# A fused linear-attention and mixer kernel: seven weight shifts written in place, loads and ranks in a new order

## The chip, the cores and the metric

One NeuronCore of a Trainium2 chip runs the whole program. The time is device microseconds of that core, lower is better. The engines are TensorE (PE, with its weight loads listed as PEld), VectorE (DVE), ScalarE (ACT), GpSimd (POOL) and SyncE (SP), which here only issues DMAs. Each engine runs its own instructions strictly in the order in which the program was written; engines wait for each other by semaphores.

## The reference

Batch 4, 4 heads, 1088 positions, head dimension 32. A linear attention with a product feature map of 8 x 8 = 64 features is followed by a token mixer and a channel mixer:

```
phi(x) = outer(S1 x, S2 x)                         # 64 features of q and of k
x   = (phi(q) @ (phi(k)^T v)) / (phi(q) @ sum_s phi(k) + 1e-6)     # [B, 1088, 128]
u   = x + (relu(x^T @ w_tok1) @ w_tok2)^T          # token mixer, 256 hidden
out = u + relu(u @ w_ch1) @ w_ch2                  # channel mixer, 1536 hidden
```

Data are float32; S1, S2 and the four weights arrive as float64 words (two 32 bit words each) and are turned into float32 on the chip.

## The kernel before, in words

**Conversion of weights.** Each weight is cut into pieces: w00 to w04 (w_tok1), w10 to w15 (w_tok2), w20 to w22 (w_ch1), w30 to w32 (w_ch2), seventeen in all, and `s` for S1 and S2. `convert` makes float32 from a piece in six operations: `.abs` (ACT, L363, high word into a buffer `c`), `.low` (ACT, L367, low word into `tail`), `.clamp` (DVE, L370, `c` to `c`), `.shift` (DVE, L374, `c` shifted left by 3 and masked, into a PSUM bank of the pool `ps_h`), `.merge` (DVE, L377, puts the sign bit in, from the high word and the PSUM bank back to `c`), and `.add` (POOL, L381 and L383, `c` plus `tail`). Pieces of w_tok are kept as `whole`; each piece is then split into a high half (`.hi`, ACT, L474) and a low half (`.lo`, POOL or DVE, L477), so that TensorE can work with three fast products in place of one slow one. `c` and `tail` have four buffers each, `ps_h` three banks, which the channel mixer uses too.

**Batches.** For each batch b: keys `K` (projection L504, feature products k_p on DVE L534, sums with v L551, block matrix `kvz` L561), queries `Q` (batch 0 on PE, L642; later ones through DRAM, L697, L714 to L740), attention and token mixer `A` (L760 and the division L768 to L778; L816 or L822 with w_tok1; the relu `h` L834; its transposition L856; the residual L847; L938 or L942 with w_tok2; `uh` and `ul`, the halves of u, L913 and L916). In batch 0 the token mixer uses `whole` float32 weights, later batches the halves.

**Channel mixer.** `U0` to `U11` are spans of up to 384 positions. For each span and each of 12 hidden blocks: three matmuls with w_ch1 into a `ps_h` bank (L992), the relu on ACT (`hh`, L996), the rest of it on DVE (`hl`, L999), three matmuls with w_ch2 into a `ps_o` bank (L1005). These 144 blocks are most of the time.

**What sets the order.** The operations are put into a list with names (`w13.clamp`, `K1.s`, `U0.h`); `Plan.run` walks through them with a rough cost for each and gives the next one on whichever engine is free to the operation of the highest level. The level is the cost of all that depends on it plus a number of its own from the table `LEAD` (in ns). Loads are issued by SP in the order of `LOADS`. Where it believes PE idle, the program puts in matmuls of an identity (`fill`, L342) whose results nobody reads. An operation with `port=True` is kept apart in this plan from POOL's operations; that concerns the plan alone, on the chip the engines' queues and semaphores decide.

Of the kernel before, what the change touches and what calls it, by code (L numbers as in the profile page):

```python
# [11 lines left out]
I32 = mybir.dt.int32  # L12
# [18 lines left out]
TILES = tuple((t * P, P) for t in range(NT))  # L31

CUTS = {0: (2, 2, 2, 2, 1), 2: (4, 4, 4), 3: (4, 4, 4)}
LOADS = "k0 q0 00 v0 01 02 03 04 10 11 20 30 q1 12 13 k1 21 31 v1 14 15 22 32".split()


WIDE = 384
# [2 lines left out]
def _spans():  # L40
# [22 lines left out]
KEYS_ON_POOL = set()  # L63

LEAD = {
    "A0.d2": -161700.0,
    "A0.u0": -740800.0,
    "A0.w2": 67900.0,
    "A1.n2": 62000.0,
    "A1.x": 384700.0,  # L70
    "A1.xT3": 472400.0,
    "A2.w0": -38700.0,
    "A2.w1": -1729700.0,
    "A3.w2": -107200.0,
    "K0.kvz": -142200.0,
    "K0.s08": -237500.0,
    "K1.s": -160000.0,
    "K1.v0": 40800.0,
    "K3.c0": 99700.0,
    "K3.p": 103300.0,  # L80
    "K3.s": -300900.0,
    "K3.v4": -498400.0,
    "Q0.a10": 1269000.0,
    "Q0.a20": 461800.0,
    "Q1.m00": -332100.0,
    "Q1.m10": -30800.0,
    "Q1.p": 115700.0,
    "Q3.p": -1683600.0,
    "U0.f": 988300.0,
    "U0.h": 359200.0,  # L90
    "U0.l": -79900.0,
    "U1.f": 653600.0,
    "U11.f": 345700.0,
    "U2.f": 96300.0,
    "U2.l": -115500.0,
    "U2.s": -804700.0,
    "U4.l": 520500.0,
    "U5.s": -35900.0,
    "U6.s": -144500.0,
    "U8.s": -175400.0,  # L100
    "w00.hi": -357200.0,
    "w00.lo": -624600.0,
    "w00.low": 15500.0,
    "w01.add": -162900.0,
    "w01.hi": -266600.0,
    "w01.lo": -1103500.0,
    "w02.hi": -337700.0,
    "w02.lo": -1981200.0,
    "w03.hi": -871700.0,
    "w03.lo": -604900.0,  # L110
    "w03.low": 376600.0,
    "w03.shift": -580100.0,
    "w04.abs": 1406800.0,
    "w04.add": 140400.0,
    "w04.hi": -260600.0,
    "w04.lo": -663100.0,
    "w04.low": 1049700.0,
    "w10.abs": 830500.0,
    "w10.hi": -265000.0,
    "w10.low": 172800.0,  # L120
    "w10.shift": -115500.0,
    "w11.abs": 656200.0,
    "w11.clamp": -128400.0,
    "w11.low": -9800.0,
    "w12.abs": 1523900.0,
    "w12.clamp": -157100.0,
    "w12.hi": -811900.0,
    "w12.lo": -452800.0,
    "w12.low": 1313100.0,
    "w13.abs": 945800.0,  # L130
    "w13.clamp": -534800.0,
    "w13.hi": 621700.0,
    "w13.low": -19300.0,
    "w13.merge": 637100.0,
    "w13.shift": -290300.0,
    "w14.lo": -1439000.0,
    "w14.low": -519800.0,
    "w15.clamp": 19000.0,
    "w15.low": -641500.0,
    "w21.clamp": 156100.0,  # L140
    "w21.low": -51800.0,
    "w22.abs": 140100.0,
    "w30.clamp": 716200.0,
    "w30.low": -55000.0,
    "w31.hi": -429100.0,
    "w32.low": -49100.0,
}


# [8 lines left out]
SWITCH = 175.0  # L158
STICK = 3000.0


LEAST = 2.0 ** -15
MOST = 122879.9921875
# [2 lines left out]
def f32(ap):  # L166
    return ap.bitcast(F32)
# [119 lines left out]
def act_sb(n):  # L287
    return {"act": 100 + 0.834 * n}


def dve(n):
    return {"dve": 69 + 1.042 * n}


def dve2(n):
    return {"dve": 69 + 0.521 * n}
# [7 lines left out]
def attn_mixer_kernel(ctx: ExitStack, tc: tile.TileContext, qT, kT, v1, s64, wt1, wt2, wc1, wc2, out):  # L304
# [8 lines left out]
    plan = Plan(bufs)  # L313

    def new(tag, shape, dtype=F32):
        return pool.tile(shape, dtype, name=tag, bufs=bufs.get(tag, 1))

    def bank(tag):
        return psum.tile([P, 512], F32, name=tag, bufs=bufs[tag])
# [33 lines left out]
    def convert(name, raw, n, loaded, dst=None, keep=None):  # L353


        t = {}
        c_hold, tail_hold, ps_hold = keep or Hold("c"), Hold("tail"), Hold("ps_h")
        words = raw.bitcast(I32).rearrange("p (n t) -> p n t", t=2)
        low, high = words[:, :, 0], words[:, :, 1]

        def magnitude(_):
            t["c"] = const.tile([P, n], I32, name="s_c") if keep else new("c", [P, CONV], I32)[:, :n]
            nc.scalar.activation(f32(t["c"]), f32(high), AF.Abs)  # L363

        def rest(_):
            t["tail"] = new("tail", [P, CONV], I32)[:, :n]
            nc.scalar.activation(t["tail"], low.bitcast(U32), AF.Copy, scale=2.0 ** -29)  # L367

        def clamp(_):
            nc.vector.tensor_scalar(f32(t["c"]), f32(t["c"]), LEAST, MOST, op0=ALU.max, op1=ALU.min)  # L370

        def shift(_):
            t["ps"] = bank("ps_h").bitcast(I32)[:, :n]
            nc.vector.tensor_scalar(t["ps"], t["c"], 3, 0x3FFFFFFF, op0=ALU.logical_shift_left, op1=ALU.bitwise_and)  # L374

        def merge(_):
            nc.vector.scalar_tensor_tensor(t["c"], high, -(1 << 30), t["ps"], op0=ALU.bitwise_and, op1=ALU.bitwise_or)  # L377

        def add(e):
            if dst:  # L380
                engines[e].tensor_tensor(dst(), t["c"], t["tail"], op=ALU.add)  # L381
            else:
                engines[e].tensor_tensor(t["c"], t["c"], t["tail"], op=ALU.add)  # L383

        a = plan.add(name + ".abs", act_sb(n), magnitude, [loaded], [c_hold])
        r = plan.add(name + ".low", act_sb(n), rest, [loaded], [tail_hold])
        m = plan.add(name + ".clamp", dve2(n), clamp, [a], (), [c_hold], port=True)
        m = plan.add(name + ".shift", dve(n), shift, [m], [ps_hold], [c_hold])
        m = plan.add(name + ".merge", dve(n), merge, [m], (), [c_hold, ps_hold])
        ways = {"dve": 69 + 2.084 * n} if keep else {"pool": 141 + 2.15 * n}  # L390
        m = plan.add(name + ".add", ways, add, [m, r], (), [c_hold, tail_hold], port=True)
        return m, t, c_hold
# [44 lines left out]
    by_kind = {"q": (load_q, q_loaded), "k": (load_k, k_loaded), "v": (load_v, v_loaded)}  # L437
    for name in LOADS:
        if name[0] in by_kind:
# [3 lines left out]
        else:  # L443
            w, i = int(name[0]), int(name[1])
            doubles[w, i] = const.tile([P, pieces[w, i].shape[1]], I64, name=f"doubles{w}{i}", tag=f"weight{w}{i}")
            prev = loaded[w, i] = load("d" + name, lambda t=doubles[w, i]: t, pieces[w, i], P * 8 * pieces[w, i].shape[1], [prev])

    s_done, s_t, _ = convert("s", s_raw, 64, s_loaded, None, Hold("s_c"))


# [600 lines left out]
    for b in range(B):  # L1051
# [60 lines left out]
```

## Time and profile before

| what | value |
|---|---|
| three runs, us | 223.5, 221.6, 222.46 (median 222.46) |
| profiled execution, us | 223.0 |
| its span, us | 220.8 |
| instructions in the span | 4921 |
| granted TensorE clock | 0.998 |
| busy: PE, DVE, ACT, POOL | 212.9 (96%), 138.6 (63%), 118.0 (53%), 80.3 us (36%) |

The span is the time between the first and the last instruction that the profiler saw; the execution's own time is 2.2 us longer. Busy shares are averages over stages that differ: DVE is busy 97 to 100% between 20 and 40 us and about half of the time behind 100 us. PE's busy time contains the filling matmuls.

### The profile page before, as it was taken

The page shows a single profiled execution, that of the slowest core. Times are in us where ns is not written, and L with a number is a line of the kernel's source. Part 1 is how long each engine was busy: PE and PEld are TensorE (multiplying, and loading weights), DVE is VectorE, ACT ScalarE, POOL GpSimd, SP SyncE. Part 2 cuts the span into 40 slices and gives each one's busy share as a digit, 9 for nine tenths or more (in the row PEclk, how much of TensorE's full clock was granted, in tenths as well). Part 3 has the DMA queues.
Part 4 walks back from the last instruction along what each step waited for, and adds up shares of the span by engine and source line. Part 5 has one row for each costly group of instructions (what it writes and reads, how often), then busy time and mean ns, then how long its engine had stood idle before and what let it go on. Part 6 is the DMA issues. An engine that isn't in the chain of part 4 may idle for free.

```text
span 220.8 us, 4921 instructions
## 1 busy us (share of the span) xinstructions
PE 212.9 (96%) x1898; PEld 201.6 (91%) x1898; DVE 138.6 (63%) x273; ACT 118.0 (53%) x284; POOL 80.3 (36%) x85
## 2 busy tenths in 40 slices
PE   7898999998999999999999999999999999999994
PEld 7677669888998999999999899999999999999993
DVE  1589999889648466555744355558255645556562
ACT  4497799996436145443443554455235545445551
POOL 2067597997999103840500240544002210000000
PEclk9999999999999999999999999999999999999999
DMA  6999996994103898510060258400610100100000
GB/s 180 368 409 408 403 399 214 198 208 150 37 3 118 246 221 166 146 67 0 3 228 22 63 136 152 180 0 6 210 38 0 39 1 0 36 3 36 0 33 24
DMA packets 11351, 28.42 MB, mean 129 GB/s; under 512 B 1472, under 2 KB 5568, under 8 KB 11328
## 3 DMA queue, kind: packets, MB, share of 16 engines
q1 hardware_dynamic: 11328, 28.11, 41.5%
q8 instruction: 15, 0.25, 0.5%
q14 instruction: 8, 0.07, 0.1%
HBM read 23.27 MB, written 4.83 MB: 127 GB/s over the span
## 4 chain that ended last, share of the span: by engine, by line
PE 79%; ACT 8%; DVE 5%; DMA 4%; issue 2%; SPq 1%; DVEq 0%; ACTq 0%
PE ps_h L992 30%; PE ps_o L1005 30%; PE ps_a L822 4%; PE ps_a L942 4%; DMA doubles<-wt 4%; PE ps_a L760 3%; PE ps_a L551 2%; ACT halves L474 2%; DVE c L370 2%; ACT tail L367 2%; ACT hh L996 2%; PE ps_a L504 2%; PE ps_a L816 1%; ACT c L363 1%; PE ps_a L938 1%
## 5 line engine op out<-in xcount | busy, mean ns | idle before, releaser
L999 DVE SCALAR_TENSOR_TENSOR hl<-ps_h,hh 128x384 fp32r<-128x384 f32 (+2 forms) x144 | 75.5, 534 | 51.3 <-ACT hh L996 47.4
L996 ACT ACTIVATE hh<-ps_h 128x384 fp32r<-128x384 f32 (+2 forms) x144 | 67.6, 474 | 60.4 <-PE ps_h L992 37.3
L992 PE MATMUL ps_h<-uh,halves 128*128 128x384 f32 (+2 forms) x288 | 88.6, 334 | 0.8 <-DVE hl L999 0.7
L1005 PE MATMUL ps_o<-hh,halves 128*128 128x384 f32 (+2 forms) x288 | 70.7, 328 | 0.0
L992 PEld LDWEIGHTS ps_h<-uh,halves 128*128 128x128 f32 x288 | 53.1, 187 | 3.0 <-DVE hl L999 1.6
L1005 PEld LDWEIGHTS ps_o<-hh,halves 128*128 128x128 f32 x288 | 50.7, 188 | 0.5 <-ACT hh L996 0.4
L1005 PE MATMUL ps_o<-hl,halves 128*128 128x384 f32 (+2 forms) x144 | 47.2, 328 | 0.0
L992 PE MATMUL ps_h<-ul,halves 128*128 128x384 f32 (+2 forms) x144 | 47.1, 327 | 0.0
L916 POOL TENSOR_TENSOR ul<-us,uh 128x64 fp32r<-128x64 f32 (+4 forms) x15 | 9.6, 652 | 51.8 <-ACT uh L913 51.7
L1005 PEld LDWEIGHTS ps_o<-hl,halves 128*128 128x128 f32 x144 | 27.0, 188 | 0.3 <-DVE hl L999 0.3
L992 PEld LDWEIGHTS ps_h<-ul,halves 128*128 128x128 f32 x144 | 27.1, 188 | 0.2
L740 POOL TENSOR_TENSOR qp<-qp,br 128x544 f32<-128x544 f32 x12 | 16.2, 1370 | 10.8 <-DMA br<-rows 10.7
L534 DVE TENSOR_TENSOR k_p<-ps_a,a_sb 128x1024 f32<-128x1024 f32 (+1 forms) x12 | 11.0, 953 | 7.1 <-ACT a_sb L514 7.1
L788 POOL TENSOR_TENSOR xl<-x,xh 128x384 fp32r<-128x384 f32 x9 | 9.0, 1020 | 15.2 <-ACT den L768 14.3
L381 POOL TENSOR_TENSOR whole<-c,tail 128x512 int32<-128x512 int32 (+3 forms) x11 | 11.9, 1090 | 4.1 <-DVE c L377 2.6
L367 ACT ACTIVATE tail<-doubles 128x512 int32<-128x512 uint32 (+3 forms) x17 | 10.4, 622 | 2.8 <-DMA doubles<-wt 2.8
L477 POOL TENSOR_TENSOR halves<-whole,halves 128x384 fp32r<-128x384 f32 (+3 forms) x11 | 11.5, 1063 | 0.0
L342 PEld LDWEIGHTS ps_o<-ident 128*128 128x128 f32 x60 | 8.9, 227 | 2.8 <-POOL ident masks.py:199 1.4
L363 ACT ACTIVATE c<-doubles 128x512 f32<-128x512 f32 (+3 forms) x17 | 10.5, 626 | 1.5 <-DMA doubles<-wt 1.1
L342 PE MATMUL ps_o<-ident 128*128 128x128 f32 x60 | 9.7, 318 | 1.4 <-POOL ident masks.py:199 1.4
L377 DVE SCALAR_TENSOR_TENSOR c<-doubles,ps_h 128x512 int32<-128x512 int32 (+3 forms) x17 | 10.3, 611 | 0.1
L374 DVE TENSOR_SCALAR ps_h<-c 128x512 int32<-128x512 int32 (+3 forms) x17 | 10.3, 618 | 0.1
(76 smaller groups left out, 230.2 us busy)
## 6 DMA issues: line engine op xcount, KB each, us to landing
qp<-rows SPq DMA_DIRECT2D x6, 544.0 KB, 9.1
br<-rows SPq DMA_DIRECT2D x12, 272.0 KB
doubles<-wc SPq DMA_DIRECT2D x6, 512.0 KB
v_sb<-v SPq DMA_DIRECT2D x4, 594.0 KB
q_sb<-qT SPq DMA_DIRECT2D x4, 544.0 KB, 12.1
doubles<-wt SPq DMA_DIRECT2D x4, 512.0 KB, 8.6
k_sb<-kT SPq DMA_DIRECT2D x3, 576.0 KB, 6.0
xm<-xb SPq DMA_DIRECT2D x3, 576.0 KB, 2.7
```

The costliest lines, as they stand in the source:

```text
L342: nc.tensor.matmul(spare_ps[:, :P], lhsT=ident, rhs=ident, start=True, stop=True)
L363: nc.scalar.activation(f32(t["c"]), f32(high), AF.Abs)
L367: nc.scalar.activation(t["tail"], low.bitcast(U32), AF.Copy, scale=2.0 ** -29)
L374: nc.vector.tensor_scalar(t["ps"], t["c"], 3, 0x3FFFFFFF, op0=ALU.logical_shift_left, op1=ALU.bitwise_and)
L381: engines[e].tensor_tensor(dst(), t["c"], t["tail"], op=ALU.add)
L477: engines[e].tensor_tensor(halves[w, i][:, 1], f32(whole[w, i] if w < 2 else t["c"]), f32(halves[w, i][:, 0]), op=ALU.subtract)
L534: engines["pool" if on_pool else "dve"].tensor_tensor(t["k_p"][:pn, t0 * H:t1 * H], a.unsqueeze(3).broadcast_to([pn, n, R, R]), t["sb", t0 ...
L740: engines[e].tensor_tensor(qp[:, p, cs], qp[:, p, cs], t["br"][:, p, cs], op=ALU.mult)
L992: nc.tensor.matmul(h_ps[:, :cn], lhsT=part(2, at[2][e][0], l, at[2][e][1] * P, P), rhs=r[:, :cn], start=(m == 0), stop=(m == 2))
L996: nc.scalar.activation(t["hh"][:, :cn], t["h"][:, :cn], AF.Relu)
L999: nc.vector.scalar_tensor_tensor(t["hl"][:, :cn], t["h"][:, :cn], 0.0, f32(t["hh"][:, :cn]), op0=ALU.max, op1=ALU.subtract)
L1005: nc.tensor.matmul(outs[i][:, :cn], lhsT=part(3, at[3][e][0], l, at[3][e][1] * P, P), rhs=r[:, :cn], start=(e == 0 and m == 0), stop=(e == ...
```

## The change

Three things change. A set `IN_PLACE` names seven of the eighteen conversions; their shift is written to `c` itself instead of a `ps_h` bank, and does not take such a bank. `LOADS` has a new order. The table `LEAD` is replaced as a whole. The line numbers behind the table move by one (L992 becomes L991, L374 becomes L372, L370 becomes L366).

```
-LOADS = "k0 q0 00 v0 01 02 03 04 10 11 20 30 q1 12 13 k1 21 31 v1 14 15 22 32".split()
+LOADS = "q0 k0 00 v0 01 03 04 02 10 13 11 20 12 q1 k1 v1 30 15 21 32 22 31 14".split()
...
-    "w13.clamp": -534800.0,
+    "w13.clamp": 14800.0,
...
+IN_PLACE = {"s", "w00", "w04", "w10", "w15", "w22", "w31"}
...
+        in_place = name in IN_PLACE
+
         def shift(_):
-            t["ps"] = bank("ps_h").bitcast(I32)[:, :n]
+            t["ps"] = t["c"] if in_place else bank("ps_h").bitcast(I32)[:, :n]
             nc.vector.tensor_scalar(t["ps"], t["c"], 3, 0x3FFFFFFF, op0=ALU.logical_shift_left, op1=ALU.bitwise_and)
...
-        m = plan.add(name + ".shift", dve(n), shift, [m], [ps_hold], [c_hold])
-        m = plan.add(name + ".merge", dve(n), merge, [m], (), [c_hold, ps_hold])
+        m = plan.add(name + ".shift", dve2(n) if in_place else dve(n), shift, [m], [] if in_place else [ps_hold], [c_hold], port=in_place)
+        m.alt = (dve2(n), True) if not in_place else (dve(n), False)
+        m = plan.add(name + ".merge", dve(n), merge, [m], (), [c_hold] if in_place else [c_hold, ps_hold])
```

(`m.alt` is read nowhere.) What moves shows in the engines' orders. First DVE from batch 0's second query product (`qp` of 320 columns) to the first division (RECIPROCAL): `c` and `ps_h` carry buffer numbers, `doubles` the name of the piece. Before:

```order
L670 TENSOR_TENSOR qp_75<-xT_192,ps_h_227 128x320
L370 TENSOR_SCALAR c_232<-c_232 128x512
L370 TENSOR_SCALAR c_249<-c_249 128x512
L374 TENSOR_SCALAR ps_h_278<-c_232 128x512
L377 SCALAR_TENSOR_TENSOR c_232<-doubles01_84,ps_h_278 128x512
L370 TENSOR_SCALAR c_282<-c_282 128x512
L370 TENSOR_SCALAR c_286<-c_286 128x256
L670 TENSOR_TENSOR qp_75<-xT_192,ps_h_268 128x384
L374 TENSOR_SCALAR ps_h_303<-c_249 128x512
L374 TENSOR_SCALAR ps_h_306<-c_286 128x256
L377 SCALAR_TENSOR_TENSOR c_249<-doubles02_85,ps_h_303 128x512
L377 SCALAR_TENSOR_TENSOR c_286<-doubles04_87,ps_h_306 128x256
```

In the changed kernel, from the same `qp`:

```order
L669 TENSOR_TENSOR qp_75<-xT_158,ps_h_212 128x320
L372 TENSOR_SCALAR ps_h_250<-c_218 128x512
L375 SCALAR_TENSOR_TENSOR c_218<-doubles01_84,ps_h_250 128x512
L366 TENSOR_SCALAR c_248<-c_248 128x256
L366 TENSOR_SCALAR c_274<-c_274 128x512
L372 TENSOR_SCALAR c_248<-c_248 128x256
L366 TENSOR_SCALAR c_276<-c_276 128x512
L669 TENSOR_TENSOR qp_75<-xT_158,ps_h_266 128x384
L372 TENSOR_SCALAR ps_h_293<-c_276 128x512
L372 TENSOR_SCALAR ps_h_300<-c_274 128x512
L375 SCALAR_TENSOR_TENSOR c_276<-doubles02_87,ps_h_293 128x512
```

The clamp of w01 now stands ahead of `qp`, w04 (256 columns) is shifted in place, w03 and w04 come ahead of w02, and the merge of w04 has moved behind the first division. The second place is DVE in the channel mixer of batch 0, where `hl` rows alternate with conversions. Before, the last conversions there use PSUM banks:

```order
L370 TENSOR_SCALAR c_641<-c_641 128x512
L370 TENSOR_SCALAR c_728<-c_728 128x320
L999 SCALAR_TENSOR_TENSOR hl_773<-ps_h_755,hh_772 128x384
L374 TENSOR_SCALAR ps_h_791<-c_641 128x512
L999 SCALAR_TENSOR_TENSOR hl_786<-ps_h_768,hh_785 128x384
L377 SCALAR_TENSOR_TENSOR c_641<-doubles32_99,ps_h_791 128x512
```

In the changed kernel w31, w22 and w15 are shifted in place there, two of them one behind the other, and the key products `k_p` of batch 2 follow:

```order
L366 TENSOR_SCALAR c_749<-c_749 128x320
L372 TENSOR_SCALAR c_632<-c_632 128x512
L372 TENSOR_SCALAR c_749<-c_749 128x320
L375 SCALAR_TENSOR_TENSOR c_632<-doubles22_97,c_632 128x512
L375 SCALAR_TENSOR_TENSOR c_749<-doubles15_94,c_749 128x320
L998 SCALAR_TENSOR_TENSOR hl_775<-ps_h_757,hh_774 128x384
L998 SCALAR_TENSOR_TENSOR hl_785<-ps_h_768,hh_784 128x384
L998 SCALAR_TENSOR_TENSOR hl_794<-ps_h_777,hh_793 128x384
L533 TENSOR_TENSOR k_p_813<-ps_a_725,a_sb_781 128x1024
```

What moved: the keys of batch 2 stood behind the attention of batch 1 and now stand ahead of it. PE shows the same. In the changed kernel, in the channel mixer of batch 0:

```order
L1004 MATMUL ps_o<-hh,halves_596 128x384 x2
L1004 MATMUL ps_o<-hl,halves_596 128x384
L503 MATMUL ps_a<-s_c,k_sb 64x64 x18
L991 MATMUL ps_h<-uh,halves_686 128x384
L991 MATMUL ps_h<-ul,halves_686 128x384
```

Here L503, the key projection of batch 2, stands between w30's and w21's blocks; before, it stood between blocks of 320 columns, behind the attention of batch 1. Both programs hold the same matmuls but for the fillers: 30 before, 27 in the changed kernel.

More of the change, by code (lines that the diff above doesn't have):

```diff
@@ L65 @@
 LEAD = {
[L66 to L130, printed above, removed]
-    "w13.clamp": -534800.0,
[L132 to L144, printed above, removed]
@@ L145 @@
-    "w31.hi": -429100.0,
-    "w32.low": -49100.0,
+    "A0.d2": -1148900.0,
+    "A0.t2": -747000.0,
+    "A0.u0": -112500.0,
+    "A0.u2": -1563800.0,
+    "A0.w2": 527000.0,
+    "A1.hT": -168800.0,
+    "A1.t1": 128100.0,
+    "A2.w0": -267200.0,
+    "A2.w2": -159800.0,
+    "A3.n0": 170600.0,
+    "A3.t1": 32000.0,
+    "A3.w0": -310300.0,
+    "A3.w1": -372400.0,
+    "A3.w2": -12000.0,
+    "K0.c0": -565700.0,
+    "K0.c8": -100000.0,
+    "K0.kvz": -1581600.0,
+    "K0.s18": -69000.0,
@@ new lines @@
+    "K0.v4": -41500.0,
+    "K1.v0": 31500.0,
+    "K2.v4": -179100.0,
+    "K3.p": 32600.0,
+    "Q0.a10": 27400.0,
+    "Q0.a21": -25800.0,
+    "Q0.b21": -4000.0,
+    "Q1.m00": -132100.0,
+    "U1.f": 43600.0,
+    "U11.s": -83100.0,
+    "U2.f": 244800.0,
+    "U2.s": -775100.0,
+    "U3.f": -33600.0,
+    "U4.h": -59900.0,
+    "U4.l": -498500.0,
+    "U5.f": 55400.0,
+    "U7.f": -11000.0,
+    "U7.s": -85600.0,
+    "U8.f": -18000.0,
+    "w00.hi": -73700.0,
+    "w00.lo": -205600.0,
+    "w01.add": -202600.0,
@@ new lines @@
+    "w01.clamp": -8300.0,
+    "w01.hi": -1141100.0,
+    "w02.low": -390500.0,
+    "w03.abs": -1055500.0,
+    "w03.hi": -13200.0,
+    "w03.lo": -1293900.0,
+    "w03.low": -296300.0,
+    "w03.merge": -770300.0,
+    "w04.hi": -586200.0,
+    "w04.merge": -636700.0,
+    "w10.hi": -524200.0,
+    "w10.lo": -209500.0,
+    "w10.shift": 222600.0,
+    "w11.low": -1217400.0,
+    "w12.clamp": 204700.0,
+    "w12.hi": 178500.0,
+    "w12.low": 24000.0,
+    "w12.merge": 36700.0,
+    "w13.abs": -312500.0,
@@ L147 @@
+    "w13.clamp": 14800.0,
+    "w13.lo": -644100.0,
+    "w13.low": -1258800.0,
+    "w13.merge": 65300.0,
+    "w14.abs": 477000.0,
+    "w14.clamp": 216300.0,
+    "w14.lo": -403400.0,
+    "w15.clamp": 102100.0,
+    "w15.lo": -1105600.0,
+    "w20.abs": -261400.0,
+    "w22.add": -117300.0,
+    "w22.clamp": 27100.0,
+    "w30.clamp": 82200.0,
+    "w31.abs": 216200.0,
+    "w32.abs": -69400.0,
+    "w32.add": -86700.0,
 }
```

## The prediction

> **What bounds the kernel now.** I first cut the span into three stretches: start-up, the rest of batch 0, and everything behind it. The columns are the busy time of PE, its weight loads (PEld), DVE, ACT and POOL with the number of their instructions, then the granted clock, the DMA share and GB/s.
>
> ```profile
> 0.00:33.00 33.00, 29.06 (x349) 23.24 (x350) 24.69 (x51) 23.48 (x59) 16.32 (x23) 1.00 0.95 361
> 33.00:62.00 29.00, 28.22 (x213) 26.04 (x211) 24.24 (x46) 22.96 (x53) 26.17 (x23) 1.00 0.59 155
> 62.00:221.00 159.00, 155.63 (x1339) 152.29 (x1337) 89.71 (x177) 71.52 (x175) 37.78 (x41) 1.00 0.28 76
> ```
>
> From 62 us on PE is busy but for the last 3.4 us behind its last matmul; DVE and ACT are busy half of that time. The two programs run the same matmuls in another order, so this stretch can only pass a gain or a loss on. The list of PE's waits says where PE stands still:
>
> ```profile
> PE ps_o L342 <- POOL ident masks.py:199: 1.4, 1, 1.4
> PE ps_a L642 <- DMA q_sb<-qT: 1.0, 1, 1.0
> PE ps_a L816 <- ACT c L363: 0.9, 1, 0.9
> PE ps_h L992 <- DVE hl L999: 0.7, 1, 0.7
> PE ps_a L847 <- DVE k_p L534: 0.3, 1, 0.3
> PE ps_a L760 <- ACT kvz L561: 0.2, 1, 0.2
> PE ps_a L856 <- ACT h L834: 0.2, 1, 0.2
> ```
>
> and the page's groups say with what it is kept busy meanwhile:
>
> ```profile
> L342 PE MATMUL ps_o<-ident 128*128 128x128 f32 x60 | 9.7, 318 | 1.4 <-POOL ident masks.py:199 1.4
> ```
>
> The waits add up to 4.7 us; the 60 instructions of L342 are dummies that fill PE's idle time, all before 33 us. The room is thus start-up (some 14 us of fillers and waits before the first L992) and one stall in the second stretch. The first L992 starts here, behind a wait of its predecessors on DVE's k_p (time, length, engine, operation):
>
> ```profile
> 27.17 0.37 ACT L834 ACTIVATE h<-ps_a 128x256 f32<-128x256 f32 x1
> 30.48 1.23 DVE L534 TENSOR_TENSOR k_p<-ps_a,a_sb 128x1024 f32<-128x1024 f32 x1
> 31.76 0.55 PE L847 MATMUL ps_a<-ident,x 128*128 128x128 f32 x3 [0.33 <-DVE k_p L534]
> 33.14 0.63 PE L992 MATMUL ps_h<-uh,halves 128*128 128x384 f32 x1
> ```
>
> **The shifts themselves.** What a shift costs on DVE with its result in PSUM, and the clamp (the same kind of instruction, SBUF to SBUF):
>
> ```profile
> L374 DVE TENSOR_SCALAR ps_h<-c 128x512 int32<-128x512 int32 x10 | 6.9, 689 | 0.0
> L370 DVE TENSOR_SCALAR c<-c 128x512 f32<-128x512 f32 x10 | 4.2, 434 | 2.0 <-ACT c L363 2.0
> L374 DVE TENSOR_SCALAR ps_h<-c 128x384 int32<-128x384 int32 x4 | 2.2, 556 | 0.0
> L370 DVE TENSOR_SCALAR c<-c 128x384 f32<-128x384 f32 x4 | 1.3, 352 | 0.0
> ```
>
> No int32 shift inside SBUF is in this trace. Its bounds are the clamp's time below and the PSUM form's above; I take the clamp's, since only type and operation differ. That saves 0.255 us on each of w00, w22 and w31, 0.20 on w10, by the line through these two 0.18 on w15 and 0.15 on w04, and nothing that counts on s: 1.3 us of DVE, 0.6 of it (w00, w04, w10) before the first L992. The rest lies where DVE still waits for ACT.
>
> The price is in two rows of the clamp. At 16.14 two clamps take 1.72 us, at 14.14 two take 0.76:
>
> ```profile
> 14.14 0.76 DVE L370 TENSOR_SCALAR c<-c 128x512 f32<-128x512 f32 x2
> 16.14 1.72 DVE L370 TENSOR_SCALAR c<-c 128x512 f32<-128x512 f32 x2
> 16.30 1.41 POOL L381 TENSOR_TENSOR whole<-c,tail 128x512 int32<-128x512 int32 x1 [0.40 <-DVE c L377]
> ```
>
> The second clamp of the 16.14 pair ends only after POOL's tensor_tensor, 1.0 us late. The Trainium skill, "SBUF — State Buffer", section "Who interferes with whom", says that DVE in a two-port mode and GpSimd exclude each other: whoever starts first holds the shared port pair for its whole instruction. It names tensor_scalar between SBUF operands among the takers and one with PSUM not, so it speaks against this change: by that rule seven more DVE instructions can be blocked, or block. The trace agrees for clamps (1.72 against 0.76); no run here shows it for a shift.
>
> **Start-up, step by step.** The loads: q0 goes ahead of k0, but what stands before v0, w00 and w01 is the same sum of bytes, so the two landings that release work stay:
>
> ```profile
> 10.90 0.80 PE L551 MATMUL ps_o<-v_sb,k_p 128*64 128x66 f32 x20
> 12.14 0.68 ACT L363 ACTIVATE c<-doubles 128x512 f32<-128x512 f32 x1 [0.42 <-DMA doubles<-wt]
> 18.76 2.32 PE L760 MATMUL ps_a<-kvz,qp 128*64 128x66 f32 x72 [0.20 <-ACT kvz L561]
> ```
>
> PE's wait of 1.0 us for q goes, but k0's second half, which ended the k_p work early before, now comes some 2 us later; both lie ahead of these landings, and v0 hides them: nothing. From 12.14 to the copies of kvz, which L760 waits for, ACT runs the same instructions as now in another order and never waits, so L760 starts at 18.76 as now. Then DVE decides:
>
> ```profile
> 13.73 0.49 DVE L670 TENSOR_TENSOR qp<-xT,ps_h 128x320 f32<-128x320 f32 x1 [0.86 <-ACT xT L660]
> 20.95 0.21 DVE L776 RECIPROCAL rec<-den 128x12 f32<-128x12 f32 x1
> 21.97 0.46 PE L816 MATMUL ps_a<-whole,x 128*128 128x256 f32 x1 [0.89 <-ACT c L363]
> ```
>
> Between qp and the reciprocal DVE has 7.2 us without a gap. Of these the change takes out one clamp of w01 (0.34, now ahead of qp), one merge of w04 (0.34, half of a 512 wide one's 0.69; now behind x) and 0.15 of w04's shift, so up to 0.83; the blocked clamp stays, since clamps of w04 and w03 still surround POOL's add of w01. As den of the first group is ready only behind two more ACT instructions (about 20.1), I take 0.6: L816 starts near 21.4 instead of 21.97.
>
> That is not handed on. Before h (27.17) ACT has the same nine instructions as now, and three of them wait for POOL to give back a buffer: w12.low for the add of w04, w20.low for that of w03, w13.abs for that of w10. The add of w03 ends at 23.8 in both, and w10's stays at 25:
>
> ```profile
> 22.50 1.28 POOL L381 TENSOR_TENSOR whole<-c,tail 128x512 int32<-128x512 int32 x1 [0.25 <-DVE c L377]
> 24.95 1.05 POOL L381 TENSOR_TENSOR whole<-c,tail 128x384 int32<-128x384 int32 x1 [1.17 <-DVE c L377]
> ```
>
> So w13.abs starts at about 26.05, w11.low behind it, and h at 26.95: 0.2 us earlier. w10's shift in place meets POOL's add of w03 (till 23.8) and loses what it saved. From h on the order is the old one on PE, ACT and DVE, and k_p comes 0.1 to 0.2 earlier. **First term: -0.2 us.** Bounds: -1.5, if neither the buffers nor the port hold (0.6 at x, 0.6 of shifts, 0.34 of clamp); +1.0, if one more clamp or shift waits out a POOL add (the 1.0 above; clamp w13 stands within 0.1 us of the add of w11).
>
> **Second stretch.** The one long stall of PE now is a chain that starts at the port:
>
> ```profile
> 46.77 1.83 DVE L370 TENSOR_SCALAR c<-c 128x512 f32<-128x512 f32 x2
> 46.94 1.47 POOL L740 TENSOR_TENSOR qp<-qp,br 128x544 f32<-128x544 f32 x1
> 48.52 0.54 DVE L999 SCALAR_TENSOR_TENSOR hl<-ps_h,hh 128x384 fp32r<-128x384 f32 x1
> 50.31 0.44 PE L992 MATMUL ps_h<-uh,halves 128*128 128x384 f32 x1 [0.68 <-DVE hl L999]
> ```
>
> A clamp waits for POOL, hl behind it is late, its PSUM bank comes free late, and PE stops. The orders of clamps and POOL work are new here, so this stall goes; the waits of PE's weight loads, which head each matmul, add up to 2.0 us in 33 to 64 us:
>
> ```profile
> PEld ps_h L992 <- DVE hl L999: 1.4, 2, 1.0
> PEld ps_o L1005 <- DVE hl L999: 0.3, 1, 0.3
> PEld ps_a L760 <- POOL o_sb L1021: 0.3, 1, 0.3
> ```
>
> What is late next: batch 2's key products move into this stretch, three DVE instructions, by the first row 2 x 1.22 and one a quarter as wide, at least 0.3: 2.7 us or more.
>
> ```profile
> L534 DVE TENSOR_TENSOR k_p<-ps_a,a_sb 128x1024 f32<-128x1024 f32 x8 | 9.6, 1221 | 7.1 <-ACT a_sb L514 7.1
> L999 DVE SCALAR_TENSOR_TENSOR hl<-ps_h,hh 128x384 fp32r<-128x384 f32 x108 | 59.1, 556 | 42.7 <-ACT hh L996 39.1 <-PE ps_o L1005 3.4
> ```
>
> From batch 1's k_p to batch 1's reciprocal I count on DVE 6 k_p, 18 hl, 3 ul, 6 clamps, 4 shifts to PSUM, 3 in place and 7 merges. At the times between starts (0.08 less than a row's length, as qp at 13.73 with 0.49 and the clamp at 14.14 show) that is 24 us, from 30.4 to 54.4. PE's matmuls from the first L991 to batch 1's L759, at the chain's rate below, come to 24 us as well, from 33 to 57: 2.6 us of slack for DVE, where the stretch's row now shows 4.8 idle (29 - 24.24).
>
> ```profile
> 55.34 1.06 PE ps_o L1005 x6
> ```
>
> The copies of hh wait behind more conversions on ACT, and I find one stall of 0.7 us (an hl behind w22.abs and kvz on ACT, at about 40 us) and 0.3 to 0.5 in pieces later. That makes 1.0 to 1.2, and with the 0.3 for o_sb, which stays, 1.5 for the old 2.0. **Second term: -0.5 us.** Bounds: -2.0 (no stall left) and +3 (three in-place shifts, w31, w22, w15, each blocked 1.0 like the clamp, none taken up by slack).
>
> **The sum.** The profiled execution took 223.0 us: span 220.8 and 2.2 around it. -0.2 - 0.5 gives 222.3. The runs' median, 222.46, lies 0.54 below that execution, so against it I forecast 221.8. A measurement of this kernel tells about 1% from no change, that is 220.2 to 224.7.
>
> **Rivals.** (1) *Start-up hands its gain on.* If POOL's adds follow DVE at once, x, h and k_p all come 1.5 us earlier, and with the stall of 1.0 gone and no new one the time is 222.46 - 2.5 = 220.0. For it: DVE has no idle time from 13.7 us on. Against it: three ACT instructions before h wait for POOL, not for DVE. (2) *Slower, by the port.* w31, w22 and w15 are shifted between 41 and 46 us, where POOL has adds and low halves queued; if each meets one (1.0 us) and DVE's 2.6 us of slack are used by the k_p, hl is late as at 48.52, and PE loses 3: 225.4. (This is the rule of the Trainium skill named above, taken to hold for shifts.) It decides from the second blocked instruction on; with one, slack takes it. (3) *The shift stays as slow as before* (0.69, no lock): DVE keeps its 1.3 us, start-up its 0.2 gain at most; 222.2. (4) *Nothing moves at h*, and the stalls only change places: 222.5.
>
> **Chances.** Forecast 0.45, (3) and (4) together 0.17: these lie within 1%. (1) 0.23, (2) 0.15. The low end, 219.4, takes in (1) and most of what the two lower bounds together (-3.5, 219.0) leave below it; the high end, 224.6, takes in the start-up's +1.0 with one stall of 1 us more, and leaves out (2). Faster by over 1%: 0.23; within: 0.62; slower: 0.15.
>
> **What would show it.** Right: L991's first start between 32.5 and 33.4; h at about 27; shifts of w00 near 0.42 us; no wait of 1 us at L991 for hl, k_p of batch 2 before 52 us. Wrong: an in-place shift of over 1 us beside a POOL row with hl late behind it (2), or h before 26 us (1). I would be wrong altogether if a load that I took as hidden (w30, five places later in LOADS) held the first L1004 back.

## The result, and the profile after

The changed kernel takes **225.14 us** (median of four runs, 224.44 to 226.96) beside 222.34 for the kernel before on the same chip (221.6 to 223.5). The ratio is 1.014, with a 95% interval from 1.010 to 1.019: slower by 2.8 us. A second comparison gave 225.28 to 222.37, ratio 1.016 (1.012 to 1.020). Of its ten executions in the two comparisons the three with a mean granted clock of 0.992 took 226.6 to 227.0 us, the other seven 224.4 to 225.5. The forecast was 221.8; the second rival, "slower, by the port", had 225.4.

The profiled execution took 224.44 us, its span is 222.5. The same three stretches as before, with the same columns (PE, PEld, DVE, ACT, POOL, granted clock, DMA share, GB/s):

```profile
0.00:33.00 33.00, 29.62 (x348) 23.38 (x349) 25.10 (x52) 24.33 (x60) 16.93 (x24) 1.00 0.95 363
33.00:62.00 29.00, 25.98 (x297) 22.74 (x295) 25.80 (x41) 20.54 (x51) 23.57 (x20) 1.00 0.67 198
62.00:222.50 160.50, 157.34 (x1250) 155.31 (x1249) 90.46 (x182) 73.14 (x175) 39.45 (x43) 1.00 0.23 67
```

In the second stretch PE is busy for 25.98 us where it was 28.22, and DVE for 25.80 where it was 24.24. PE's list of waits names the place:

```profile
PE ps_h L991 <- DVE hl L998: 2.1, 1, 2.1
PE ps_h L991 <- DVE c L375: 0.7, 1, 0.7
```

One wait of 2.1 us for an `hl`, where before it was 0.7, and a new kind: a channel matmul waits for a merge (L375), which gives a `ps_h` bank back. No wait of PE for a load is listed behind the first L991, so the later load of w30 is not the cause. The start-up came out early instead (time, length, engine, operation):

```profile
11.44 0.68 ACT L359 ACTIVATE c<-doubles 128x512 f32<-128x512 f32 x1 [1.27 <-DMA doubles<-wt]
19.54 0.22 DVE L775 RECIPROCAL rec<-den 128x12 f32<-128x12 f32 x1
26.25 0.39 ACT L833 ACTIVATE h<-ps_a 128x256 f32<-128x256 f32 x1
32.06 0.63 PE L991 MATMUL ps_h<-uh,halves 128*128 128x384 f32 x1
```

The first L991 is at 32.06 (33.14 before). From it to the end of the span there are 190.4 us in this kernel and 187.7 in the one before. What fills the difference is DVE and POOL between 41 and 51 us:

```profile
41.95 1.32 POOL L476 TENSOR_TENSOR halves<-c,halves 128x512 fp32r<-128x512 f32 x1
42.03 1.53 DVE L372 TENSOR_SCALAR c<-c 128x512 int32<-128x512 int32 x1
44.70 1.28 POOL L381 TENSOR_TENSOR c<-c,tail 128x512 int32<-128x512 int32 x1 [1.43 <-DVE c L375]
45.01 1.15 DVE L366 TENSOR_SCALAR c<-c 128x320 f32<-128x320 f32 x1
45.94 1.37 POOL L476 TENSOR_TENSOR halves<-whole,halves 128x512 fp32r<-128x512 f32 x1
46.08 2.85 DVE L372 TENSOR_SCALAR c<-c 128x512 int32<-128x512 int32 x2
47.27 1.48 POOL L476 TENSOR_TENSOR halves<-c,halves 128x512 fp32r<-128x512 f32 x1
48.85 1.08 DVE L375 SCALAR_TENSOR_TENSOR c<-doubles,c 128x512 int32<-128x512 int32 x2
49.85 1.48 DVE L998 SCALAR_TENSOR_TENSOR hl<-ps_h,hh 128x384 fp32r<-128x384 f32 x3
50.45 0.44 PE L991 MATMUL ps_h<-uh,halves 128*128 128x384 f32 x1 [2.13 <-DVE hl L998]
```

Each of the three in-place shifts (w31 at 42.03, w22 and w15 in the pair at 46.08) begins just behind the start of a POOL instruction and ends 0.2 to 0.3 us behind its end. The `hl` behind them starts at 49.85, and PE stands for 2.13 us. Where no POOL instruction runs, an in-place shift of 512 columns takes 0.42:

```profile
10.54 0.42 DVE L372 TENSOR_SCALAR c<-c 128x512 int32<-128x512 int32 x1
```

### The profile page after: what moved, and what is told of

Its sections match the earlier page's. It is cut to its first block, busy times and chain, and to the rows that moved or that the text cites. A ratio compares the mean times of both kernels' runs of the same rounds, so it can differ in the third digit from the quotient of the medians.

```text
span 222.5 us, 4913 instructions
## 1 busy us (share of the span) xinstructions
PE 212.9 (96%) x1892; PEld 201.4 (91%) x1892; DVE 141.4 (64%) x273; ACT 118.0 (53%) x284; POOL 79.9 (36%) x85
## 4 chain that ended last, share of the span: by engine, by line
PE 77%; DVE 11%; issue 4%; DMA 4%; ACT 2%; SPq 1%; DVEq 0%
PE ps_o L1004 31%; PE ps_h L991 30%; PE ps_a L821 4%; PE ps_a L941 4%; DMA doubles<-wt 4%; DVE c L366 3%; PE ps_a L759 3%; DVE c L375 2%; PE ps_a L550 2%; DVE hl L998 2%; DVE ps_h L372 1%; DVE k_p L533 1%; SPq L342 1%; PE ps_a L815 1%; PE ps_a L696 1%
## 5 line engine op out<-in xcount | busy, mean ns | idle before, releaser
L991 PE MATMUL ps_h<-uh,halves 128*128 128x384 f32 (+2 forms) x288 | 88.0, 332 | 2.8 <-DVE hl L998 2.1
L991 PEld LDWEIGHTS ps_h<-uh,halves 128*128 128x128 f32 x288 | 53.1, 188 | 4.4 <-DVE hl L998 2.8
L991 PE MATMUL ps_h<-ul,halves 128*128 128x384 f32 (+2 forms) x144 | 47.1, 327 | 0.0
L991 PEld LDWEIGHTS ps_h<-ul,halves 128*128 128x128 f32 x144 | 27.0, 188 | 0.2
L366 DVE TENSOR_SCALAR c<-c 128x512 f32<-128x512 f32 (+3 forms) x17 | 10.0, 599 | 0.4 <-ACT c L359 0.4
L759 PEld LDWEIGHTS ps_a<-kvz,qp 128*64 128x64 f32 x288 | 8.8, 138 | 1.4 <-issue 1.4
L338 PE MATMUL ps_o<-ident 128*128 128x128 f32 x54 | 8.7, 320 | 1.4 <-POOL ident masks.py:199 1.4
L759 PE MATMUL ps_a<-kvz,qp 128*64 128x66 f32 x288 | 9.3, 223 | 0.6 <-ACT kvz L560 0.6
```

The costliest lines, as they stand in the source:

```text
L759: nc.tensor.matmul(x_ps[c:c + 64, o:o + 2 * (D + 1)], lhsT=qp[:, p, s0 + c:s0 + c + 64], rhs=kvz_all[b % 2][:, p, :2 * (D + 1)], start=Tru ...
L991: nc.tensor.matmul(h_ps[:, :cn], lhsT=part(2, at[2][e][0], l, at[2][e][1] * P, P), rhs=r[:, :cn], start=(m == 0), stop=(m == 2))
```

## The experiments

My theory, **"port"**: DVE's operations inside SBUF wait out the POOL instruction that they meet, `hl` is late behind them, PE stops. The rivals: **"moved work"** (batch 2's key products and more conversions crowd this stretch, whatever the port does), **"banks"** (conversions hold one of three `ps_h` banks too long), and **the loads**. Each kernel keeps the engines' orders of its parent and changes only where an operation writes, or what it is cut into, unless the text says otherwise. Lines of code move by a few numbers from kernel to kernel. Ratios are to the kernel before, on the same chip.

**The three late shifts into PSUM.**

```
-            t["ps"] = t["c"] if in_place else bank("ps_h").bitcast(I32)[:, :n]
+            t["ps"] = t["c"] if name in {"s", "w00", "w04", "w10"} else bank("ps_h").bitcast(I32)[:, :n]
```

> The changed kernel with the shifts of w31, w22 and w15 into PSUM banks again, every engine's order as in the changed kernel. Theory 'port' (DVE's in-place shifts and the clamps wait out the POOL instruction they meet, hl comes late, PE stops): the three shifts take 0.70, 0.70 and 0.49 us instead of 1.53, 1.51 and 1.42, PE's stall of 2.3 us at 48 us goes, the stall of 0.8 at 38.5 us, which stands behind a blocked clamp, stays; about 2 us less, 223.1. Theory 'moved work' (batch 2's key products and more conversions crowd DVE and ACT there, the blocks are taken up by slack): the stall at 48 us stays within 0.5 us, 224.8. Third: a shift now waits for one of three ps_h banks and the stall moves; 224 to 226.

Measured: 223.47 (10 runs), ratio 1.007 (1.004 to 1.010). From the first L991 to the end 188.9 us instead of 190.4. The shift of w31 stands against the same POOL instruction and is not held:

```profile
42.53 1.32 POOL L476 TENSOR_TENSOR halves<-c,halves 128x512 fp32r<-128x512 f32 x1
42.60 0.68 DVE L372 TENSOR_SCALAR ps_h<-c 128x512 int32<-128x512 int32 x1
45.80 1.07 DVE L372 TENSOR_SCALAR ps_h<-c 128x512 int32<-128x512 int32 x2
47.52 0.44 PE L991 MATMUL ps_h<-uh,halves 128*128 128x384 f32 x1 [0.99 <-DVE c L375]
```

The wait for `hl` of 2.1 us is gone, so "port" holds and "moved work" falls for this stall: the key products stand where they stood. In its place PE waits 0.99 us for the bank of a merge; that the stall moves was the third expectation, though it had 224 to 226. The three in-place writes cost 1.5 us net in the trace and 1.7 in the medians; the second comparison's interval (1.012 to 1.020) lies clear of this one's (1.004 to 1.010).

**One of them alone in place (w31).**

```
+            t["ps"] = t["c"] if name in {"s", "w00", "w04", "w10", "w31"} else bank("ps_h").bitcast(I32)[:, :n]
```

> The changed kernel with w22 and w15 shifted into PSUM banks and only w31 left in place among the late ones (w31 meets POOL's low half of w21 at 42 us and is blocked). The prediction's rule 'one blocked instruction is taken up by slack': as with all three in PSUM, 223.5. If each blocked instruction costs its own 0.8 us: 224.2.

Measured: 224.33 (6 runs), ratio 1.011 (1.008 to 1.014), from the first L991 to the end 190.2 us, in an execution of 225.12 us, 0.8 above the median. One blocked shift is not taken up:

```profile
42.88 1.52 DVE L372 TENSOR_SCALAR c<-c 128x512 int32<-128x512 int32 x1
45.86 1.17 DVE L366 TENSOR_SCALAR c<-c 128x320 f32<-128x320 f32 x1
47.94 1.07 DVE L375 SCALAR_TENSOR_TENSOR c<-doubles,ps_h 128x512 int32<-128x512 int32 x2
48.66 0.44 PE L991 MATMUL ps_h<-uh,halves 128*128 128x384 f32 x1 [1.37 <-DVE c L375]
```

w31's late merge holds POOL's add back, which then meets the clamp of w15 (1.17 us; 0.39 in the experiment above), and the merges behind it give the banks back late. One block makes the next.

**All seven into PSUM, loads and ranks alone.**

```
+            t["ps"] = t["c"] if name in () else bank("ps_h").bitcast(I32)[:, :n]
```

> The changed kernel with all seven shifts into PSUM banks, every engine's order as in the changed kernel: new loads and ranks alone. If the in-place shifts gave the start-up its 1.1 us, the first L991 starts 0.6 us later than in the changed kernel (w00 0.27, w04 0.13, w10 0.20), at 32.7; if the loads and the order gave it, at 32.1 to 32.3. Theory 'port': no stall of 2 us near 48 us; total 223.1 to 223.7. Theory 'moved work': the stalls stay, 224.9 to 225.6.

Measured: 223.48 (10 runs), ratio 1.005 (1.003 to 1.008). The first L991 is at 33.68, later than either expectation. By the landing of w01 (11.60 us here) it comes 22.08 us behind it, where the changed kernel has 20.62: two clamps in the start-up now wait out POOL instructions at new places:

```profile
15.57 1.90 DVE L366 TENSOR_SCALAR c<-c 128x256 f32<-128x256 f32 x2
17.73 0.96 DVE L366 TENSOR_SCALAR c<-c 128x512 f32<-128x512 f32 x1
```

(1.90 for two that take 0.8 alone, 0.96 for one of 0.42.) In the second stretch no clamp of w31 or w14 is held here, and from the first L991 to the end there are only 187.9 us, 1.0 less than with the late shifts alone in PSUM, where both are held. One wait of 1.36 us for the bank of a merge remains, at 47.80. So in this one trace about half of the loss against the kernel before lies in the start-up (the first L991 is 0.6 us later than the mean of before's three profiles), and the rest of the span is 1 us shorter where those clamps are not held.

**The seven in place in the kernel before, its order kept.**

```
-            t["ps"] = bank("ps_h").bitcast(I32)[:, :n]
+            t["ps"] = t["c"] if name in {"s", "w00", "w04", "w10", "w15", "w22", "w31"} else bank("ps_h").bitcast(I32)[:, :n]
```

> The kernel before with the seven shifts in place, every engine's order, loads and ranks as before: the in-place writing alone. Theory 'port': w00, w04 and w10 save up to 0.6 us before the first L992, but in the second stretch POOL works at the places of the late shifts (42.8, 49.1 and 51.2 us), so two or three of them take over 1 us instead of 0.7 or 0.5 and hl is late behind them: PE loses 0 to 2 us more than before, 222.0 to 224.3. Theory 'moved work': the in-place shifts can only help, 221.9 to 222.5. The landings of the first loads (v0 at 10.9, w01 at 12.14 us) are as in the kernel before, if the load order set them.

Measured: 223.93 (10 runs), ratio 1.008 (1.005 to 1.012). Writing in place makes this order slower as well, and not only in the second stretch. In the start-up the *merge* behind the shift is held, because with the shift in place both its inputs lie in SBUF (0.69 us for the same merge from a PSUM bank):

```profile
12.01 0.42 DVE L374 TENSOR_SCALAR c<-c 128x512 int32<-128x512 int32 x1
12.35 1.01 POOL L667 TENSOR_TENSOR qp<-xT 128x384 f32<-128x384 f32 x1 [10.59 <-ACT xT L660]
12.46 1.45 DVE L377 SCALAR_TENSOR_TENSOR c<-doubles,c 128x512 int32<-128x512 int32 x1
```

The first L992 comes 21.7 us behind w01's landing (21.0 before). My expectation counted no loss in the start-up. Taken singly, the loads and ranks cost 0.5% (the experiment above) and the in-place writes 0.8%; both together, the whole change, cost 1.4 to 1.6%. Within the intervals the two halves add up.

**POOL's instruction cut into four.** The low halves of w21, w01 and w31 are made in pieces of 128 columns.

```
+            step = n // 4 if name in {"w21", "w01", "w31"} else n
+            for j in range(0, n, step):
+                engines[e].tensor_tensor(...[:, j:j + step], op=ALU.subtract)
```

> The changed kernel with POOL's low halves of w21, w01 and w31 (the three that the in-place shifts of w31, w22 and w15 meet) each cut into four instructions of 128 columns; the shifts stay in place, same order otherwise. Theory 'port' with one hold for each POOL instruction: a shift waits for at most one piece (about 0.4 us) and then gets in, so each takes 0.4 to 0.9 us instead of 1.4 to 1.5 and PE's stall at 48 us shrinks to under 1 us; about 1.5 us less, 223.5, unless POOL's extra starts make it late. If the block lasts until POOL has no more work queued, or if something else than POOL's instruction makes the shifts long, they stay at 1.4 to 1.5 and the time at 225.

Measured: 223.67 (10 runs), ratio 1.008 (1.005 to 1.011).

```profile
42.41 2.38 POOL L478 TENSOR_TENSOR halves<-c,halves 128x128 fp32r<-128x128 f32 x4
42.50 0.68 DVE L372 TENSOR_SCALAR c<-c 128x512 int32<-128x512 int32 x1
46.15 0.91 DVE L372 TENSOR_SCALAR c<-c 128x512 int32<-128x512 int32 x2
```

w31's shift, which starts 0.09 us behind POOL's first piece, takes 0.68 instead of 1.53. So the hold lasts for one POOL instruction, not for its queue. (w22's and w15's shifts take 0.91 together instead of 2.85, but POOL's pieces start behind them here, at 46.23, so they test it less.) PE's wait for `hl` shrinks to 0.89 us, and the time comes out near the 223.5 expected. The four pieces take 2.38 us instead of 1.32: POOL waits for DVE in turn.

**Clamps out of SBUF as well.** The three late shifts go into PSUM as in the first experiment. For w31, w14, w22 and w15 the clamp writes into the bank as well, and stands right ahead of the shift on DVE (a part of the edit):

```
+            if name in {"w31", "w14", "w22", "w15"}:
+                nc.vector.tensor_scalar(f32(t["ps"]), f32(t["c"]), LEAST, MOST, op0=ALU.max, op1=ALU.min)
```

> The changed kernel without any clamp or shift inside SBUF between 33 and 50 us: for w31, w14, w22 and w15 the clamp writes from c into the PSUM bank right ahead of the shift, which works inside that bank; s, w00, w04 and w10 stay in place, other engines' orders as in the changed kernel. Theory 'port', that blocked clamps (w31 1.24, w14 1.16 us) also caused the stalls in which a channel matmul waits for a bank that a merge gives back late: none of these instructions takes over 0.75 us, the stalls of 1.6 us that were left with the three shifts in PSUM go, from the first L991 to the end 187.3 us instead of 188.9, time 221.3 to 221.8. Rival 'banks': conversions that hold one of three banks cost PE these stalls whatever the port does; 223.2 to 223.7.

Measured: 223.12 (10 runs), ratio 1.007 (1.004 to 1.010); again, in a later comparison, 223.11 (6 runs), 1.006 (1.004 to 1.008).

> The kernel with w31, w14, w22 and w15 clamped into PSUM, unchanged, beside the one with k0 first: the first L991 at 32.1 to 32.7 us, from there to the end 188.8, 223.1, 0.6% above before.

No clamp or shift is held in the stretch, yet from the first L991 to the end there are 188.8 and 188.6 us, no less than with the shifts alone moved. "Banks" was right here: a stall of 1.5 us remains behind a merge.

```profile
43.82 0.68 DVE L374 TENSOR_SCALAR ps_h<-c 128x512 f32<-128x512 f32 x1
44.53 0.70 DVE L375 TENSOR_SCALAR ps_h<-ps_h 128x512 int32<-128x512 int32 x1
45.14 0.48 DVE L374 TENSOR_SCALAR ps_h<-c 128x320 f32<-128x320 f32 x1
45.66 0.50 DVE L375 TENSOR_SCALAR ps_h<-ps_h 128x320 int32<-128x320 int32 x1
46.80 0.44 PE L994 MATMUL ps_h<-uh,halves 128*128 128x384 f32 x1 [1.54 <-DVE c L378]
```

Two conversions stand one behind the other: w22 holds a bank from 43.82, w15 a second one from 45.14, and PE gets one back only with the merges behind them, just before 46.80.

**The same with w15's three instructions behind the next three `hl`** (DVE's order is changed at this one place).

> As the one with w31, w14, w22 and w15 clamped into PSUM (stall of 1.7 us at 45 us behind w22's and w15's six instructions, w22's merge giving its bank back last), and w15's three instructions moved behind the next three hl on DVE. If the order on DVE between the hl's is what is left of the loss: w22's merge ends 0.85 us earlier and hl does not wait behind w15, the stall shrinks to under 0.9, about 222.3. If the banks are short whatever the order: the stall moves to w15's merge, 223.1.

Measured: 223.57 (10 runs), ratio 1.007 (1.005 to 1.010). The stall shrinks as foretold, the time does not:

```profile
46.62 0.45 PE L1003 MATMUL ps_h<-uh,halves 128*128 128x384 f32 x1 [0.30 <-DVE c L387]
57.95 0.84 PEld L949 LDWEIGHTS ps_a<-whole,hTl 128*128 128x128 f32 x4 [0.63 <-POOL whole L391]
57.95 1.34 PE L949 MATMUL ps_a<-whole,hTl 128*128 128x320 f32 x4 [0.38 <-POOL whole L391]
```

POOL, which adds the pieces in a fixed order, waits for w15's merge; everything behind it comes later, w14's add among it, and the token mixer of batch 0's last 320 positions waits for that at 57.95:

```profile
50.18 0.88 POOL L391 TENSOR_TENSOR whole<-c,tail 128x320 int32<-128x320 int32 x1 [1.96 <-DVE c L387]
57.05 0.85 POOL L391 TENSOR_TENSOR whole<-c,tail 128x320 int32<-128x320 int32 x1
```

The weight loads, which head the matmuls, wait 0.63 us there, and 0.29 us for another result of POOL at 57.13. Together that is what the edit had won: counted from the first channel matmul, batch 2's `kvz` is copied 0.87 us earlier than without this edit (22.95 instead of 23.82), the next `uh` at the same time (26.66 and 26.64). From the first channel matmul to the end: 188.9.

**w03's clamp out of SBUF too**, in the start-up (name added to the set of the kernel with clamps in PSUM).

> As the one with w31, w14, w22 and w15 clamped into PSUM, and w03 as well, whose clamp waits out POOL's add of w01 at 15.5 us (1.06 to 1.49 us instead of 0.42). If the start-up hands a gain of DVE on: the reciprocal 0.4 to 0.8 us earlier against w01's landing, the first L991 as much, 220.7 to 221.2. If ACT's conversions that wait for POOL's buffers decide: the first L991 at most 0.2 us earlier, 221.2 to 221.7.

Measured: 223.75 (10 runs), ratio 1.009 (1.006 to 1.011), so no gain. The first L991 is 20.98 us behind w01's landing, 20.63 without this edit: the POOL add that held w03's clamp now holds the next SBUF instruction, w04's in-place shift (1.25 us, 0.28 alone):

```profile
14.93 1.30 POOL L382 TENSOR_TENSOR whole<-c,tail 128x512 int32<-128x512 int32 x1
15.13 1.25 DVE L375 TENSOR_SCALAR c<-c 128x256 int32<-128x256 int32 x1
```

**The two held clamps of the kernel before out of SBUF** (`w04` and `w14`, the same edit in the old order).

> The kernel before with the two clamps that its trace shows blocked (w04 at 16.49 us, 1.37; w14 at 47.11 us, 1.49) written into the PSUM bank right ahead of the shift; orders otherwise as before, no shift in SBUF. Theory 'port': the stall of 0.7 us at 50 us goes, and the start-up gains 0.1 (ACT and POOL decide) to 0.9 us (DVE decides): 220.5 to 221.3. If the port costs this kernel nothing: 222.0.

Measured: 221.67 (10 runs), ratio 0.999 (0.997 to 1.002): nothing that can be measured. The first L992 came 20.51 us behind w01's landing (21.00 before), but the hold went on to the clamp of w15 (1.36 us; 0.32 in the profile of before, at 53.20):

```profile
52.56 1.31 POOL L480 TENSOR_TENSOR halves<-c,halves 128x512 fp32r<-128x512 f32 x1
52.70 1.36 DVE L371 TENSOR_SCALAR c<-c 128x320 f32<-128x320 f32 x1
```

Two more profiles of the kernel before show another part of why.

> The kernel before, unchanged, profiled a second time. Its first profiled execution took 223.0 us, 0.95 and 1.26 above the medians of 31 and 25 later runs (222.05, 221.74). If that execution started late by chance (w01 landed at 12.14 us), this one shows the first L992 at 32.2 to 32.8 and takes about 222; the time from the first L992 to the end stays at 187.7. If not, 33.1 and 223 again.

> The kernel before, unchanged, profiled a third time, with runs of its own: from the first L992 to the end 187.3 to 187.7. If the two traces so far show executions with late loads (its runs' medians lie 0.2 to 1.2 us below them): w01 lands before 12 us here and the first L992 is near 32.5. If not: 33.1 again.

The second profile (222.56 us) repeats the first: w01 lands at 12.16, the first L992 starts at 33.17, with 187.3 us behind it and the same stall (0.70). The third (221.78 us, the median of its 12 runs; ratio to the others 1.000, 0.998 to 1.003) has the same start-up, 32.96, but 186.7 us behind it instead of 187.7. The late landing that I suspected is not the cause (11.95 us). It is the clamp of w14, which here is not held:

```profile
46.57 0.65 DVE L370 TENSOR_SCALAR c<-c 128x512 f32<-128x512 f32 x2
47.17 1.37 POOL L740 TENSOR_TENSOR qp<-qp,br 128x544 f32<-128x544 f32 x1 [0.48 <-DMA br<-rows]
33.00:62.00 29.00, 28.91 (x245) 27.11 (x245) 24.07 (x48) 23.30 (x53) 26.88 (x25) 1.00 0.62 154
```

POOL's product waited 0.48 us for a DMA, the clamp got in ahead of it, and the stall of 0.7 us did not come: PE is busy for 28.91 of 29 us. So the kernel before has this stall in some executions and not in others, and the trace from which I predicted was one with it.

**The load order.** First q0 ahead of k0 in the kernel before, then k0 ahead of q0 in the new order (with the clamps in PSUM); only these three DMAs change places.

> The kernel before with the load of q0 issued ahead of the two of k0, nothing else moved. If the order of these three sets when w00 and w01 land (w01 at 11.4 to 12.0 us in the four kernels with q0 first, 12.1 and 12.7 in the two with k0 first): w01 lands at 11.4 to 12.0, the first L992 about 0.5 earlier, 221.5. If landings only vary from run to run: 222.0, and w01 anywhere between 11.4 and 12.7.

> The changed kernel without clamps and shifts in SBUF between 33 and 50 us (w31, w14, w22, w15 clamped into PSUM), and with the two loads of k0 ahead of q0 as in the kernel before; nothing else moved. In the kernel before, q0 first cost 2.0 us although w01 landed no later. If the load order is what holds all kernels of the new order 1.4 us above before: about 222, the first L991 near 31.5. If PE's first instructions, which here need q0, wait instead: q0's wait moves every later step of the start-up by 0.5 to 1 us, 223.6 to 224.2.

Measured: 223.72 (4 runs), ratio 1.011 (1.005 to 1.017), the first L992 at 34.06; and 226.50 (4 runs), ratio 1.021 (1.018 to 1.024), the first L991 at 35.93, 3.4 us over its parent where I expected 0.5 to 1. PE's order fits one load order each. The first row is from the old order with q0 first, the second from the new order with k0 first:

```profile
7.74 0.80 PE L512 MATMUL ps_a<-s_c,k_sb 128*64 128x64 f32 x20 [1.08 <-DMA k_sb<-kT]
7.94 1.65 PE L652 MATMUL ps_a<-q_sb,s_spread 64*128 64x384 f32 x4 [1.95 <-DMA q_sb<-qT]
```

In the old order with q0 first the key projections, which come first on PE there, wait 1.6 us in all for k0. In the new order with k0 first the query projections wait till 7.94, the key projections queue behind them, and the sums with v start at 14.91 instead of 10.34 and 10.94 in the parent's two profiles. The order of q0 and k0 is thus not what holds the new order above before; the rest of the new `LOADS` was not tested alone.

## Why the prediction was wrong

**Start-up (first term, -0.2): the size was right, the reason only in part.** Counted from the landing of w01, the reciprocal came 0.71 earlier (8.81 to 8.10 us; forecast 0.6), `h` 0.22 (15.03 to 14.81; forecast 0.2), the first L991 0.38 (21.00 to 20.62; forecast 0.2). So rival (1), that start-up hands its gain on, did not happen: between the division and `h` two thirds of the gain were lost, as forecast. But what lost them in the trace is not ACT's wait for POOL's buffers:

```profile
22.50 1.56 PE L815 MATMUL ps_a<-whole,x 128*128 128x256 f32 x6 [0.40 <-DVE x L777]
24.78 0.67 ACT L705 COPY abT<-ps_a 128x272 f32<-128x272 f32 x2 [0.94 <-PE ps_a L696]
25.34 0.58 ACT L359 ACTIVATE c<-doubles 128x384 f32<-128x384 f32 x1
```

The second `x` stands on DVE behind two merges, PE waits for it, and ACT's last wait ahead of `h` is for PE. The gate that I named is close by, but it did not decide here: POOL's add of w10 ended at 25.27, and w13.abs began at 25.34, behind the copies of `abT`. That the two paths end within 0.1 us of each other, so that the size came out, is luck. Two more statements were wrong. The shift of w10 was not held (0.35 us at 23.09). And "the two landings" did not "stay": w01 lands at 12.14, 12.16 and 11.95 us in three profiles of before (12.68 and 12.41 in two other kernels with its order and loads), and between 11.41 and 12.10 (mean 11.68) in the ten profiles of kernels with the new order and its loads, about 0.4 earlier than in before. Together the first L991 of the changed kernel lies at 32.06 and 32.45, 0.84 earlier on average than the three of before. Why the same bytes land sooner was not separated: with q0 first in the old order w01's conversion starts at 11.94 without a wait for its load, so it had landed by then.

**Second stretch (second term, -0.5): wrong by 3.3 to 4.2 us.** It measured +2.8 against the profile that I used (187.7 to 190.4) and +3.7 against the third one, at its runs' median (186.7). The step that failed is "one stall of 0.7 us ... at about 40 us" and "0.3 to 0.5 in pieces later". I took each DVE instruction at its unhindered time, and kept the held ones for a bound and a rival. In the measure that I used, the waits of PE's weight loads between 33 and 64 us, I put 1.5 in place of 2.0 (2.2 with a fourth wait of 0.2 that I left out). The changed kernel's list adds up to 5.7, and its two longest entries are:

```profile
PEld ps_h L991 <- DVE hl L998: 2.8, 2, 2.4
PEld ps_h L991 <- DVE c L375: 1.0, 1, 1.0
```

A stall near 40 us did come (0.67 at 39.52), but for the bank of a merge behind w14's held clamp, not for an `hl` behind ACT.

- Rival (2)'s price of a block held: 1.1 us for the shifts of 512 columns (1.53 against 0.42). That its 225.4 came so close to 225.14 is in part luck: the three blocks cost 1.5 to 1.7 us net, not 3, and the rest of the loss, which seems to stand at banks, it did not have. "It decides from the second blocked instruction on; with one, slack takes it" did not hold: with w31 alone in place the trace lost 1.3 us against none (190.2 to 188.9) and the median 0.9, though the two ratios' intervals still overlap.
- The 2.6 us of slack were an average over 24 us. PE lives on three banks here and needs an `hl` within a block or two; DVE was idle for 3.2 us of this stretch (29 - 25.80) while PE stood still for three.
- I counted in-place shifts only. In the changed kernel four clamps between 33 and 46 us were held as well (the two longest 1.24 and 1.16), and those also delayed merges, whose banks L991 waits for.
- "The orders of clamps and POOL work are new here, so this stall goes": a new order draws new meetings. A stall that this stretch had by chance was credited to the change.

**The sum.** By the means of the profiles, three of before and two of the changed kernel, -0.84 at the first L991 and +3.16 behind it give +2.3; the runs' medians differ by 2.80 and 2.91. The 0.54 by which the profiled execution lay above the median would fit the one stall of 0.7, which some executions have and others not, but it is not shown: the second profile has the stall too and lies 0.19 above its median.

**What accounts for the loss.** Shown: the late in-place shifts cost 1.5 us in the trace and 1.7 in the medians (225.14 to 223.47). Not settled is the rest, 1.2 to 1.4 us in the medians of the kernels with the new order and the late shifts in PSUM (223.1 to 223.6; 2.0 with w03's clamp moved as well). Where it stands can be read from the traces. The listed waits of PE's weight loads between 33 and 64 us add up to 2.2, 2.1 and 1.1 us in the three profiles of before, to 4.2 with the late shifts in PSUM, 3.5 with all seven there, 4.1 with the clamps out as well. The waits for the bank of a merge are 2.3, 1.7 and 2.1 of these, and none in the three profiles of before. So the banks are the likely rest, and not the port alone: with the clamps out of SBUF nothing is held in the stretch, and there are 188.8 us for 188.9. The one cure that was tried, w15's conversion placed later, took 1.2 us of the bank's stall away and lost it again through POOL's fixed order. No kernel here has the new order without a stall at a bank.

**The prices.** The in-place shift at the clamp's time was right, so rival (3) is out: 0.42 us for 512 columns (0.69 into PSUM), 0.28 for 256, 0.35 for 384. The signs I named hold for w00's shift (0.42) and for batch 2's k_p ahead of 52 us (51.25); "no wait of 1 us at L991 for hl" failed (2.13), and "an in-place shift of over 1 us beside a POOL row with hl late behind it" is what came. Of the fixed places, h (26.25) and the first L991 (32.06) were too late in my forecast by the landing.

The Trainium skill, "SBUF — State Buffer", section "Who interferes with whom", lets the side that comes first keep the shared ports for its whole instruction. The traces agree for int32 shifts (0.42 to 1.53) and show the cut: with POOL's instruction in four, 0.68. The same section of the Trainium skill lets a DVE instruction with two SBUF inputs contend with a POOL instruction that reads SBUF; the merge behind an in-place shift agrees (0.69 to 1.45).

## What to carry to other kernels

When an operand moves from PSUM into SBUF, reprice not only that instruction but every instruction that reads the result, and look up what POOL has running at that place: here both the shift and the merge behind it became things that a POOL instruction can hold for its whole length. Where a pool of three buffers couples the engines, slack counts between two handovers, not over a stretch, and a held instruction passes its delay to the engine that holds it next. Before a stall in one profile is counted as removable, take a second profile of the same kernel: if its cause is who came first by a tenth or two of a microsecond, it may be in one execution and not in the next.

## What the runs showed that I had not expected

- Taking one DVE instruction away from a POOL instruction hands the hold to the next one: w03's clamp (1.06) freed, w04's shift held (1.25 instead of 0.28).
- The hold costs POOL too: four pieces that meet DVE took 2.38 us, while four that met nothing took 0.46 each.
- The execution of the kernel before in which POOL's product waited 0.48 us for a DMA was the shorter one, by 0.6 to 0.9 us from the first L992 on: DVE's clamp came ahead of that product.
